# Two decode layers on one core: wo's last page in two transfers, and the gate's half without u done first

## The chip, the core and the metric

The kernel runs on one core of one Trainium2 chip. The metric is the device time of one execution in microseconds (us). Lower is better.

## What is computed

One token goes through two layers that share all weights. Each layer is an attention block over a key and value cache, and then a gated feed-forward block; both have a layernorm ahead and a residual around them:

```python
x = x + A(layernorm(x), k_cache, v_cache, wq, wo)
x = x + B(layernorm(x), w1, w3, w2)
x = x + A(layernorm(x), k_cache, v_cache, wq, wo)
x = x + B(layernorm(x), w1, w3, w2)

# A: 32 heads of 192, the last 4096 of 32768 cached positions, D = 640
q = x @ wq;  p = softmax(q . k * 192**-0.5);  out = concat(p . v) @ wo
# B: F = 1536
gate = x @ w1;  up = x @ w3;  out = (silu(gate) * up) @ w2
```

All data are bfloat16. Keys and values of the window are 1.5 MB a head each.

## The kernel before

**Memory.** `arena` holds 16 slots of one page, 128 x 6144 bf16 (1.5 MB). One list, `loads`, names all transfers of both layers in the order in which they are used: wq, the pages of keys and values, six pages of wo, then w1 (`fa`), w3 (`fb`), a mixed page `fc` (rest of w1, rest of w3, four chunks of w2) and `fd` (five more chunks of w2). The function `refill` takes the next entry whenever a slot is free and issues it on SP's queue; `done(key)` gives a slot back and calls it. The last three chunks of w2 (`keep`) and the last three chunks of wo's rows (`wo5`) are loaded in layer 0 and stay for layer 1. In layer 1, fourteen heads' keys are still on the chip. Each transfer on SP's queue waits, besides its slot, for the landing of the eighth transfer before it.

**Attention.** TensorE makes the scores of four heads in one accumulator, the softmax turns them, and the values are multiplied six heads later. `combine` leaves 48 columns in `otd`, one for each chunk of 128 rows of wo. `wo_proj` multiplies chunk after chunk into two accumulators, `y_ps`, four column groups at a time. Page w of six holds nine chunks, and the last page three. `y_to_residual` adds the result into `xsq`, and `layernorm` makes `xs` out of it.

**Feed-forward.** In `ffn`, `g_ps` collects x @ w1 and `u_ps` x @ w3: first four chunks of g (page `fa`), four of u (`fb`), then the fifth of g and of u (`fc`). Both are copied into `w20` as `gu`, g by ScalarE and u by VectorE, and are turned by three small matmuls each with `sel4` as the moving operand, into `gt_ps`, 24 columns of the one PSUM bank that `m_ps` lies in. Then VectorE and ScalarE make silu(g) * u out of it, in `htd`, twelve columns, one for each chunk of w2. In layer 0 the chunks of w2 are multiplied into `y2_ps`. In layer 1 `last_rows` does it: ten f32 matmuls bring the residual (`xw`, filled by GpSimd) into `f_ps`, 48 matmuls add the chunks of w2 in four column groups (a four of matmuls for each chunk), one cast follows, and the output leaves on SP's queue.

**What sets the order.** `pin` keeps every instruction in the order of the program on its engine, and `mm` does so for matmuls; all matmuls have the line of that helper, L80. So an engine runs what the code lists, in that order, and waits where its next instruction must. The framework adds the waits between engines, by what each instruction reads and writes.

The lines of the profile that matter here: L247 and L248 are the casts of y_ps, L242 writes xs, L444 and L445 are the copies of g and u, L451 is the exponential, L454 and L456 the copy into `ut` and the product `gut`, L458 and L459 the sum and the reciprocal, L460 writes `htd`, L489 is the last cast, L491 the output, and L210 issues pages.

Of the kernel before, what the change touches and what calls it, by code (L numbers as in the profile page):

```python
# [15 lines left out]
P = 128  # L16
# [31 lines left out]
def kernel(  # L48
# [79 lines left out]
    ptm = cst.tile([P, 16 * PW], BF16, name="ptm")  # L128
    otd = cst.tile([P, 48], BF16, name="otd")
    htd = cst.tile([P, 12], BF16, name="htd")  # L130
    zero = cst.tile([P, 32], BF16, name="zero")
    nc.gpsimd.memset(zero[:], 0.0)
    w20 = cst.tile([P, 768], BF16, name="w20")
    qt_sb = cst.tile([P, H, 6], BF16, name="qt_sb")
# [28 lines left out]
    for layer in range(2):  # L163
        for c in range(NCH):
            loads.append((("q", layer, c), [(0, PGW, wq_v[c])]))
        for i in range(H + LEAD):
            for kind, g, cache in (("v", i - LEAD, A_v_cache), ("k", i, A_k_cache)):
                if not 0 <= g < H:
                    continue
                h = head(layer, g)  # L170
                if kind == "k" and layer == 1 and h in RETAIN:
                    if h == STASH:
                        loads.append((("k", 1, h), []))
                    continue
                loads.append(((kind, layer, h),
                              [(0, PGW, cache[0, h, S0:SK, :].rearrange("(p t) d -> p (t d)", p=P))]))
        for w in range(6):
            parts = []
            for at, ci in enumerate(wo_order(layer)[9 * w:9 * w + 9]):
                blk, e = ORDER[layer][ci // 12], ci % 12  # L180
                if parts and parts[-1][2] == blk and parts[-1][3] + parts[-1][1] == e:
                    parts[-1][1] += 1
                else:
                    parts.append([at, 1, blk, e])
            parts = [(640 * at, 640 * n, wo_v[blk][:, 640 * e:640 * (e + n)]) for at, n, blk, e in parts]
            if w < 5:
                loads.append((("o", layer, w), parts))
            elif layer == 0:
                assert len(parts) == 1 and parts[0][1] == 1920
                loads.append((None, [(wo5[:], parts[0][2])]))  # L190
        loads.append((("fa", layer), [(0, PGW, w1_v[:, 0:PGW])]))
        loads.append((("fb", layer), [(0, PGW, w3_v[:, 0:PGW])]))
        loads.append((("fc", layer), [(0, 1536, w1_v[:, PGW:]), (1536, 1536, w3_v[:, PGW:]),
                                      (3072, 2560, w2_v[:, 0:2560])]))
        fd = [(0, 3200)] if layer == 0 else [(0, 1280), (1280, 1280), (2560, 640)]
        loads.append((("fd", layer), [(o, n, w2_v[:, 2560 + o:2560 + o + n]) for o, n in fd]))
        if layer == 0:
            loads.append((None, [(keep[:], w2_v[:, 5760:7680])]))
# [197 lines left out]

    def wo_proj(layer):
        y_ps = y_open("y_ps")
        for w in range(6):
            pg = page(("o", layer, w)) if w < 5 else wo5  # L400
            for cc, ci in enumerate(wo_order(layer)[9 * w:9 * w + 9]):
                n = 9 * w + cc
                j = n % 4
                for nh in range(2):
                    mm(y_ps[nh][32 * j:32 * j + 1, 0:320], lhsT=otd[:, ci:ci + 1],
                       rhs=pg[:, 640 * cc + 320 * nh:640 * cc + 320 * nh + 320],
                       start=False, stop=(n >= 44), tile_position=(0, 32 * j))
            if w < 5:
                done(("o", layer, w))
        y_to_residual(y_ps)  # L410
# [6 lines left out]
    def ffn(layer):  # L417
        if layer == 1:
            assert not loads
            spare = free[0] * PGW  # L420
            ident = arena[:, spare:spare + 64].bitcast(F32)
            nc.gpsimd.memset(ident, 0.0)
            for j in range(4):
                nc.gpsimd.affine_select(out=ident, in_=ident, compare_op=ALU.not_equal, fill=1.0, base=-32 * j,
                                        pattern=[[-1, 32]], channel_multiplier=1)
            xw = arena[:, spare + 64:spare + 64 + 1280].bitcast(F32)
            nc.gpsimd.memset(xw, 0.0)
            for j in range(4):
                nc.gpsimd.tensor_copy(out=xw[32 * j:32 * j + 32, 32 * j:640:128], in_=xsq[32 * j:32 * j + 32, 0:NCH])
            ident = (ident, xw)  # L430
        g_ps = ps_a.tile([P, 512], F32, tag="a", name="g_ps")
        u_ps = ps_a.tile([P, 512], F32, tag="a", name="u_ps")
        for ps, kind, c0, c1, off in ((g_ps, "fa", 0, 4, 0), (u_ps, "fb", 0, 4, 0),
                                      (g_ps, "fc", 4, 5, 0), (u_ps, "fc", 4, 5, 1536)):
            pg = page((kind, layer))
            for c in range(c0, c1):
                for j in range(4):
                    mm(ps[32 * j:32 * j + 32, 0:384], lhsT=xs[:, c, 3:35],
                       rhs=_ap(pg, 0, P, off + 1536 * (c - c0) + 3 * j, [[12, 128], [1, 3]]),
                       start=(c == 0), stop=(c == NCH - 1), tile_position=(0, 32 * j))  # L440
            if kind != "fc":
                done((kind, layer))
        gu = w20.rearrange("p (g n) -> p g n", g=2)
        pin(nc.scalar.copy(out=gu[:, 0, :], in_=g_ps[:, 0:384]))  # L444
        pin(nc.vector.tensor_copy(out=gu[:, 1, :], in_=u_ps[:, 0:384]))  # L445
        gt_ps = m_ps[:, 0:24].rearrange("p (g k j) -> p g k j", g=2, k=3)
        for gi in range(2):
            for k in range(3):
                mm(gt_ps[:, gi, k, :], lhsT=gu[:, gi, k:384:3], rhs=sel4[:], start=True, stop=True)
        ex = sml.tile([P, 12], F32, tag="ex", name="ex")  # L450
        pin(nc.scalar.activation(out=ex[:], in_=gt_ps[:, 0, :, :].rearrange("p k j -> p (k j)"), func=ACTF.Exp,  # L451
                                 scale=-1.0))
        ut = sml.tile([P, 12], F32, tag="ut", name="ut")
        pin(nc.vector.tensor_copy(out=ut[:], in_=gt_ps[:, 1, :, :].rearrange("p k j -> p (k j)")))  # L454
        gut = sml.tile([P, 12], F32, tag="gut", name="gut")
        pin(nc.vector.tensor_tensor(out=gut[:], in0=gt_ps[:, 0, :, :].rearrange("p k j -> p (k j)"), in1=ut[:],  # L456
                                    op=ALU.mult))
        pin(nc.vector.tensor_scalar_add(out=ex[:], in0=ex[:], scalar1=1.0))  # L458
        pin(nc.vector.reciprocal(out=ex[:], in_=ex[:]))  # L459
        pin(nc.vector.tensor_tensor(out=_ap(htd[:], 0, P, 0, [[1, 3], [3, 4]]),  # L460
                                    in0=gut[:].rearrange("p (k j) -> p k j", k=3),
                                    in1=ex[:].rearrange("p (k j) -> p k j", k=3), op=ALU.mult))
        if layer == 1:
            return last_rows(ident)
        y_ps = y_open("y2_ps")
        for fcx in range(12):
            j = fcx % 4
            pg, off = w2_chunk(layer, fcx)
            for nh in range(2):
                mm(y_ps[nh][32 * j:32 * j + 1, 0:320], lhsT=htd[:, fcx:fcx + 1], rhs=pg[:, off + 320 * nh:off + 320 * nh + 320],  # L470
                   start=False, stop=(fcx >= 8), tile_position=(0, 32 * j))
            if fcx == 3:
                done(("fc", layer))
        done(("fd", layer))
        y_to_residual(y_ps)

    def last_rows(ident):
        f_ps = ps_a.tile([P, 512], F32, tag="a", name="f_ps")
        eye, xw = ident
        for c in range(NCH):  # L480
            mm(f_ps[:, c:160:NCH], lhsT=xw[:, 128 * c:128 * c + 128], rhs=eye, start=(c == 0), stop=False)
        for fcx in (0, 1, 2, 3, 9, 10, 11, 4, 5, 6, 7, 8):
            pg, off = w2_chunk(1, fcx)
            for j in range(4):
                mm(f_ps[32 * j:32 * j + 1, 0:160], lhsT=htd[:, fcx:fcx + 1],
                   rhs=pg[:, off + 160 * j:off + 160 * j + 160],
                   start=False, stop=(fcx == 8), tile_position=(0, 32 * j))
        row = w20[:, 0:160]
        pin(nc.vector.tensor_copy(out=row, in_=f_ps[:, 0:160]))  # L489
        ps = row.ap[0][0]  # L490
        nc.sync.dma_start(out=out[0, 0, :].rearrange("(j i) -> j i", j=4),  # L491
                          in_=bass.AP(row.tensor, row.offset, [[32 * ps, 4], [1, 160]]))
# [69 lines left out]
```

## Time and profile before

| what | value |
|---|---|
| median of 3 runs | 528.83 us (528.5 to 529.74) |
| the profiled execution's own time | 528.32 us |
| its span | 526.6 us |
| moved by DMA | 221.97 MB, mean 421 GB/s |
| busy share of the span: PE, PEld, DVE, ACT, POOL | 52%, 21%, 49%, 12%, 3% |
| mean granted TensorE clock | 0.716 of full speed |

The span is the time from the first to the last instruction in the trace; the device time is 1.7 us longer. PE stands for TensorE's matmuls, PEld for its weight loads, DVE for VectorE, ACT for ScalarE, POOL for GpSimd and SP for the engine whose queue issues the transfers. A row of the timeline gives the start in us, the duration, engine, line, operation, output and inputs, shape and count; in brackets stand the idle time of the engine before it, and who ended it. A row of the windows gives a stretch, its length, busy time (and number of instructions) of PE, PEld, DVE, ACT and POOL, the granted clock, the share of DMA engines busy, and GB/s. In the rows of DMA queues the numbers are packets, MB and the share of 16 engines' span; in those of DMA issues, KB and the us from issue to landing.

### The profile page before, as it was taken

To read this page: it belongs to the slowest core of one execution; us is meant where nothing else is said; L and a number is where in the kernel's file an instruction comes from. 1 tells how busy PE (TensorE), PEld (TensorE's weight loads), DVE (VectorE), ACT (ScalarE), POOL (GpSimd) and SP (SyncE) were. 2 spreads that over 40 slices of the span, in tenths; PEclk is the share of its full clock that TensorE was granted. 3 is DMA by queue.
4 is the path that set the end of the run, shared out by engine and by line. 5 is a ranking of instruction groups with operands and counts; after the bars stand their busy time and mean duration, and the time that the engine had idled before them with its cause. 6 is when DMAs were issued, how large, how long until landed. Compare 5 with 4: busy or idle time off the path is not lost.

```text
span 526.6 us, 5978 instructions
## 1 busy us (share of the span) xinstructions
PE 275.0 (52%) x2403; PEld 112.6 (21%) x2403; DVE 256.4 (49%) x393; ACT 62.5 (12%) x192; POOL 16.2 (3%) x74
## 2 busy tenths in 40 slices
PE   2344644472655644455545555687254756345455
PEld 1111211131222221122112112233022322112113
DVE  1199676556657475654002139531475645753001
ACT  1002020110102020112001002022111120202000
POOL 4000000000000000000000000000000000001000
PEclk9997968666756776586556558988677886686557
DMA  8999999999999999999999999999999999999995
GB/s 349 429 430 433 426 428 427 433 432 427 427 428 432 432 426 429 428 432 423 419 431 422 427 428 427 420 431 427 428 428 431 429 428 429 429 431 428 424 432 242
DMA packets 22355, 221.97 MB, mean 421 GB/s; under 512 B 2616, under 2 KB 2744, under 8 KB 5176
## 3 DMA queue, kind: packets, MB, share of 16 engines
q1 hardware_dynamic: 22184, 221.59, 99.3%
q8 instruction: 19, 0.31, 0.2%
q14 instruction: 8, 0.07, 0.0%
q10 hardware_dynamic: 144, 0.00, 0.0%
HBM read 221.58 MB, written 0.00 MB: 421 GB/s over the span
## 4 chain that ended last, share of the span: by engine, by line
DMA 85%; PE 7%; DVE 5%; issue 1%; ACT 1%; SPq 1%; DVEq 0%; ACTq 0%
DMA arena<-in_A_k_cache_dram 51%; DMA arena<-in_A_v_cache_dram 16%; DMA arena<-in_A_wo_dram 9%; DMA arena<-in_B_w_dram 6%; DMA arena<-in_A_wq_dram 3%; DVE arena L300 3%; PE s_ps L80 3%; PE o_ps L80 2%; PE y_ps L80 1%; SPq L210 1%; PE q_ps L80 1%; PE u_ps L80 0%; PE pss L80 0%; ACT w L337 0%; DVE t L322 0%
## 5 line engine op out<-in xcount | busy, mean ns | idle before, releaser
L80 PE MATMUL s_ps<-arena,wst 128*32 128x512 bf16 x768 | 153.7, 512 | 171.3 <-DVE arena L300 84.5
L300 DVE STREAM_TRANSPOSE arena<-arena 128x1536 uint32<-128x1536 uint32 x100 | 171.2, 1754 | 75.0 <-DMA arena<-in_A_k_cache_dram 74.6
L80 PE MATMUL o_ps<-arena,ptm 128*8 128x384 bf16 (+1 forms) x1024 | 113.5, 421 | 12.9 <-DMA arena<-in_A_v_cache_dram 12.9
L80 PEld LDWEIGHTS <-wst 128*32 128x32 bf16 x768 | 53.1, 115 | 256.2 <-issue 227.1
L80 PEld LDWEIGHTS <-ptm 128*8 128x8 bf16 (+1 forms) x1024 | 40.0, 99 | 49.9 <-issue 40.3
L332 ACT ACTIVATE tb<-m 32x16 f32<-32x16 f32 x16 | 3.4, 214 | 280.4 <-DVE m L329 280.4
L350 ACT COPY ptm<-w 32x64 bf16<-32x64 bf16 x80 | 23.6, 295 | 42.5 <-PE o_ps L80 39.3
L80 PE MATMUL y_ps<-arena,otd 128*1 128x320 bf16 x180 | 16.9, 459 | 15.1 <-DMA arena<-in_A_wo_dram 15.1
L80 PE MATMUL q_ps<-arena,xs 128*32 128x512 bf16 x120 | 14.5, 624 | 17.3 <-DMA arena<-in_A_wq_dram 14.7
L383 DVE SCALAR_TENSOR_TENSOR w<-pss,rl,mask 64x192 bf16<-64x192 f32 x16 | 6.7, 417 | 32.2 <-PE pss L80 32.2
L282 POOL COPY wst<-qt_sb 32x24 bf16<-32x24 bf16 x30 | 8.4, 281 | 432.7 <-PE s_ps L80 313.8
L340 DVE STREAM_TRANSPOSE w<-w 64x512 bf16<-64x512 bf16 x16 | 11.3, 705 | 14.4 <-ACT w L337 14.4
L248 DVE CAST w<-y_ps 128x320 bf16<-128x320 f32 x3 | 1.5, 490 | 34.4 <-PE y_ps L80 34.4
L322 DVE TENSOR_REDUCE t<-s_ps 64x1 f32<-64x512 f32 x16 | 10.6, 663 | 12.2 <-PE s_ps L80 12.1
L274 DVE CAST qt_sb<-pss 32x192 bf16<-32x192 f32 x2 | 0.7, 346 | 31.2 <-PE pss L80 31.2
L350 DVE COPY ptm<-w 32x64 bf16<-32x64 bf16 x48 | 9.9, 207 | 10.8 <-PE o_ps L80 9.6
L80 PEld LDWEIGHTS <-xs 128*32 128x32 bf16 x200 | 7.2, 119 | 35.7 <-issue 26.1
L355 DVE RECIPROCAL rl<-pss 64x1 f32<-64x1 f32 x16 | 2.6, 166 | 22.2 <-PE pss L80 22.2
L80 PEld LDWEIGHTS <-otd 128*1 128x1 bf16 x192 | 6.4, 103 | 25.8 <-issue 21.7
L337 ACT ACTIVATE w<-s_ps,nbt 64x512 bf16<-64x512 f32 x16 | 10.9, 682 | 5.6 <-DVE nbt L334 5.6
L376 ACT CAST w<-o_ps 128x384 bf16<-128x384 f32 x16 | 7.7, 479 | 33.0 <-PE o_ps L80 23.7
L80 PE MATMUL pss<-w,sel 128*64 128x192 bf16 x32 | 6.3, 286 | 9.5 <-ACT w L376 6.4
(82 smaller groups left out, 111.8 us busy)
## 6 DMA issues: line engine op xcount, KB each, us to landing
arena<-in_A_v_cache_dram SPq DMA_DIRECT2D x64, 1536.0 KB, 29.2
arena<-in_A_k_cache_dram SPq DMA_DIRECT2D x50, 1536.0 KB, 29.2
arena<-in_A_wq_dram SPq DMA_DIRECT2D x10, 1536.0 KB, 9.3
arena<-in_A_wo_dram SPq DMA_DIRECT2D x6, 1440.0 KB, 15.3
arena<-in_B_w_dram SPq DMA_DIRECT2D x4, 1536.0 KB, 11.1
arena<-in_A_wo_dram SPq DMA_DIRECT2D x4, 960.0 KB, 16.8
arena<-in_A_wo_dram SPq DMA_DIRECT2D x4, 480.0 KB, 21.8
arena<-in_B_w_dram SPq DMA_DIRECT2D x4, 384.0 KB, 14.6
```

Of the source, the lines that this page charges most:

```text
L80: return pin(nc.tensor.matmul(*a, **k))
L210: pin(nc.sync.dma_start(out=arena[:, s * PGW + off:s * PGW + off + n], in_=src))
L282: pin((engs[a].copy if engs[a] is nc.scalar else engs[a].tensor_copy)(out=dst, in_=src))
L300: pin(nc.vector.transpose(x[:, w * sp:w * (sp + 1)].bitcast(U32), x[:, w * sp:w * (sp + 1)].bitcast(U32)))
L322: pin(nc.vector.reduce_max(out=t0[:, 0:1], in_=s_ps[0:64, :], axis=AX.X))
L332: pin(nc.scalar.mul(out=tb[32:64, :].rearrange("p (a z) -> p a z", a=4)[:, :, 0:HB], in_=mb, mul=-SCALE))
L337: pin(nc.scalar.activation(out=e[:], in_=s_ps[0:64, :], func=ACTF.Exp, bias=nbt[:, 0:1], scale=SCALE, accum_out=l[:]))
L340: pin(nc.vector.transpose(et[:], e[:]))
L350: pin((eng.copy if eng is nc.scalar else eng.tensor_copy)(out=dst, in_=src))
L355: pin(nc.vector.reciprocal(out=rl[half], in_=rl_ps[half]))
L376: pin(nc.scalar.copy(out=o_sb[:, 0:384], in_=o_ps[:, 0:384]))
L383: pin(nc.vector.scalar_tensor_tensor(out=om, in0=ot_ps[half], scalar=rl[half], in1=mask[half].unsqueeze(2).broadcast_to([64, 16, 12]), op0 ...
```

## The change

In layer 1 wo's page 4 (nine chunks) is loaded in two transfers, six chunks and three, into the same slot. The last page, `wo5`, which has long been on the chip, is multiplied before page 4 and not after it. In both layers the order of the gate is changed: g is copied and turned, the exponential, the sum, the reciprocal and the product g / (1 + exp(-g)) follow (into `ut`), and then u is turned and multiplied in one step from PSUM. The copy of u on VectorE still stands ahead of the gate's steps on that engine. The separate copy of u's turned half and the product `gut` are gone. In layer 1 the three kept chunks of w2 are multiplied first and not after the first four. `zero` is twice as wide.

```diff
-    zero = cst.tile([P, 32], BF16, name="zero")
+    zero = cst.tile([P, 64], BF16, name="zero")
...
+            if layer == 1 and w == 4:
+                (at, n, blk, e), = parts
+                parts = [[at, n - 3, blk, e], [at + n - 3, 3, blk, e + n - 3]]
...
-        for w in range(6):
+        for w in (0, 1, 2, 3, 4, 5) if layer == 0 else (0, 1, 2, 3, 5, 4):
             pg = page(("o", layer, w)) if w < 5 else wo5
             for cc, ci in enumerate(wo_order(layer)[9 * w:9 * w + 9]):
-                n = 9 * w + cc
+                n = 9 * w + cc if w < 4 or layer == 0 else cc + (36 if w == 5 else 39)
...
+        gu = w20.rearrange("p (g n) -> p g n", g=2)
+        gt_ps = m_ps[:, 0:24].rearrange("p (g n) -> p g n", g=2)
+        ex = sml.tile([P, 12], F32, tag="ex", name="ex")
+        ut = sml.tile([P, 12], F32, tag="ut", name="ut")
+
+        def turn(gi):
+            for k in range(3):
+                mm(gt_ps[:, gi, 4 * k:4 * k + 4], lhsT=gu[:, gi, k:384:3], rhs=sel4[:], start=True, stop=True)
+
+        def gate():
+            pin(nc.scalar.copy(out=gu[:, 0, :], in_=g_ps[:, 0:384]))
+            turn(0)
+            pin(nc.scalar.activation(out=ex[:], in_=gt_ps[:, 0, :], func=ACTF.Exp, scale=-1.0))
+            pin(nc.vector.tensor_scalar_add(out=ex[:], in0=ex[:], scalar1=1.0))
+            pin(nc.vector.reciprocal(out=ex[:], in_=ex[:]))
+            pin(nc.vector.tensor_tensor(out=ut[:], in0=gt_ps[:, 0, :], in1=ex[:], op=ALU.mult))
...
-        gu = w20.rearrange("p (g n) -> p g n", g=2)
-        pin(nc.scalar.copy(out=gu[:, 0, :], in_=g_ps[:, 0:384]))
         pin(nc.vector.tensor_copy(out=gu[:, 1, :], in_=u_ps[:, 0:384]))
-        gt_ps = m_ps[:, 0:24].rearrange("p (g k j) -> p g k j", g=2, k=3)
-        for gi in range(2):
-            for k in range(3):
-                mm(gt_ps[:, gi, k, :], lhsT=gu[:, gi, k:384:3], rhs=sel4[:], start=True, stop=True)
...
+        gate()
+        turn(1)
         pin(nc.vector.tensor_tensor(out=_ap(htd[:], 0, P, 0, [[1, 3], [3, 4]]),
-                                    in0=gut[:].rearrange("p (k j) -> p k j", k=3),
-                                    in1=ex[:].rearrange("p (k j) -> p k j", k=3), op=ALU.mult))
+                                    in0=gt_ps[:, 1, :].rearrange("p (k j) -> p k j", k=3),
+                                    in1=ut[:].rearrange("p (k j) -> p k j", k=3), op=ALU.mult))
...
-        for fcx in (0, 1, 2, 3, 9, 10, 11, 4, 5, 6, 7, 8):
+        for fcx in (9, 10, 11, 0, 1, 2, 3, 4, 5, 6, 7, 8):
```

## The prediction

> **What bounds the kernel now.** I read the page first, for who is busy all along.
>
> ```profile
> DMA  8999999999999999999999999999999999999995
> ...
> q1 hardware_dynamic: 22184, 221.59, 99.3%
> q8 instruction: 19, 0.31, 0.2%
> ```
>
> The 16 DMA engines are full from the second slice to the last half slice. So only two things can move the time: what the engines carry, and what is left after the last byte. Next come the windows of the tail, with granted clock (PEclk) and DMA share:
>
> ```profile
> 515.00:517.00 2.00, 1.35 (x16) 0.47 (x16) 0.29 (x1) 0.23 (x2) 0.00 (x0) 0.50 0.99 408
> ...
> 518.00:519.00 1.00, 1.00 (x18) 0.66 (x13) 0.00 (x0) 0.00 (x0) 0.00 (x0) 0.94 1.01 411
> ...
> 521.00:522.00 1.00, 1.00 (x10) 1.00 (x10) 0.66 (x5) 0.18 (x1) 0.00 (x0) 1.00 0.48 183
> 522.00:523.40 1.40, 1.26 (x50) 0.88 (x49) 0.18 (x1) 0.00 (x0) 0.00 (x0) 1.00 0.12 42
> ```
>
> DMA runs out between 520 and 523, and PE is full meanwhile. Which of them ends last is told by the DMA view of the last load's issue (160 KB, issued at 510.40; the last number is the us from issue to landing), and by the timeline:
>
> ```profile
> arena<-in_B_w_dram SPq DMA_DIRECT2D x1, 160.0 KB, 12.7
> ```
>
> ```profile
> 510.38 1.49 PE L80 MATMUL y_ps<-arena,otd 128*1 128x320 bf16 x17 [1.66 <-DMA arena<-in_A_wo_dram]
> ...
> 515.64 1.56 PE L80 MATMUL g_ps<-arena,xs 128*32 128x384 bf16 x16 [1.31 <-DVE xs L242]
> ...
> 517.72 1.23 PE L80 MATMUL u_ps<-arena,xs 128*32 128x384 bf16 x14 [0.52 <-DMA arena<-in_B_w_dram]
> ...
> 519.71 0.48 ACT L444 CAST w<-g_ps 128x384 bf16<-128x384 f32 x1 [4.45 <-PE g_ps L80]
> 520.14 0.56 DVE L445 CAST w<-u_ps 128x384 bf16<-128x384 f32 x1 [4.55 <-PE u_ps L80]
> ...
> 520.24 0.24 PE L80 MATMUL pss<-sel,w 128*128 128x4 bf16 x3 [0.16 <-ACT w L444]
> ...
> 520.75 0.24 PE L80 MATMUL pss<-sel,w 128*128 128x4 bf16 x3 [0.27 <-DVE w L445]
> ...
> 520.86 1.27 PE L80 MATMUL f_ps<-arena 128*128 128x32 f32 x10
> 521.03 0.18 ACT L451 ACTIVATE ex<-pss 128x12 f32<-128x12 f32 x1 [0.84 <-PE pss L80]
> ...
> 521.99 0.19 DVE L460 TENSOR_TENSOR htd<-gut,ex 128x12 bf16<-128x12 f32 x1
> 522.23 0.98 PEld L80 LDWEIGHTS <-htd 128*1 128x1 bf16 x48 [0.21 <-DVE htd L460]
> ...
> 522.72 0.65 PE L80 MATMUL f_ps<-arena,htd 128*1 128x160 bf16 x20
> 523.41 0.32 DVE L489 CAST w<-f_ps 128x160 bf16<-128x160 f32 x1 [1.23 <-PE f_ps L80]
> ```
>
> The 48 last matmuls go in twelve fours. 28 of them, seven fours, lie between 522.23 and 522.72: 0.07 us a four. The twelfth could start at 522.23 + 11 x 0.07 = 523.00. Its rows of w2 land at 510.40 + 12.7 = 523.1, and the group ends at 523.37, one matmul (0.23 by the tile's view) after 523.13. So the last transfer sets the end, with PE's chain only 0.13 us behind it. That slack decides this change.
>
> **The split of wo's page.** It adds one transfer, and no bytes. By the DMA view's landings the two-part page before it, 480 and 960 KB like the new pair, took 3.49 us (499.96 to 503.45); the whole pages after it took 3.42 (to 506.87 and 510.29). Price: 0.07 us on every later landing; bounds 0 and 0.1. One more issue on SP costs 0.33 there, and as each issue waits for the landing of the eighth transfer before it, w1's page is issued at 496.6 instead of 493.24. Its data are not due until 510.3, so this is hidden by over 10 us of queued transfers; the last load is still issued on the landing at 510.3.
>
> **Kept chunks first.** Behind the last wo landing stand 6 matmuls instead of 24, so y_ps, the layernorm and g_ps come about 1.1 us earlier (g_ps near 514.5). u_ps then still waits for its own transfer at 517.72, and the gap ahead of it grows from 0.5 to 1.7 us. Worth 0; were the cover gone, it would be 1.1. POOL's copies of the residual (done by 514.5) come earlier too, and nobody waits for them.
>
> **The gate.** Two DVE steps of 0.17 go (the copy into ut and one multiply). With the old durations and gaps: the g copy ends at 520.19, g's turn runs 520.24 to 520.48, the exponential 520.52 to 520.70. DVE is in the u cast until 520.70, then add, reciprocal and multiply (0.17, 0.23, 0.17, 0.03 apart) end at 521.37.
>
> Now what the diff does not say. In the built program the first matmul of u's turn waits, beyond its weights, for the DVE count that this multiply sets. It writes columns 12 to 23 while the multiply reads 0 to 11, of one bank: ordered, though no data need it. So u's turn starts at about 521.42, not 520.75. PE works in order, and behind it are queued the ten f32 matmuls that bring the residual into f_ps, which until now ran under the exponential. The last step on DVE follows u's turn, and htd is ready at 521.90 instead of 522.18. But PE is not free: the old rows have the first f32 matmul 0.11 us after u's turn began and the last 1.00 later (1.27 less one of 0.276), and one more step of 0.11. The w2 matmuls start at 521.42 + 1.22 = 522.64, not 522.23. Moving the kept chunks to the front covers only the landing of the others, which are in by then. The twelfth four starts at 522.64 + 0.77 = 523.41 and ends at 523.65, against 523.37: +0.28, and the bound changes from transfer to PE.
>
> **Layer 0.** The same shift makes htd about 0.3 us earlier there (288.6 to 288.3; the f32 matmuls do not exist, only two y2 openers of 0.43 in all). The w2 matmuls of that layer then wait for transfers anyway (289.45, 0.31 idle on DMA). A slot comes free 0.3 us sooner, but DMA is full there. Worth 0, and 0.3 without that cover. `zero` grows just as `gut` goes, and the arena keeps its address: 0.
>
> **Sum.** 0.07 + 0.28 = +0.35 us on the profiled 528.32 gives 528.67. The runs' median lies 0.51 above the profiled run, so 529.18, or 529.2. About 0.2% (1.06 us) is what a measurement of this kernel can tell from no change, so this counts as the same.
>
> **Rivals.**
> *The clock rises late (slower).* In the tail it goes from 0.50 to 1.00 near 518.1 (0.94 in that window). In layer 0:
>
> ```profile
> 279.00:282.50 3.50, 1.59 (x17) 0.47 (x16) 0.69 (x3) 0.41 (x2) 0.00 (x0) 0.50 0.95 402
> 282.50:286.00 3.50, 1.92 (x20) 0.82 (x21) 0.00 (x0) 0.48 (x1) 0.00 (x0) 0.50 1.05 424
> ```
>
> Sixteen such matmuls in 3.5 us did not raise it, twenty did, at 286. Before 518.1 there were also about twenty. The change pulls g_ps earlier, so about two of them leave that stretch: eighteen, between the two. If the rise comes one stretch later (near 521.5), u_ps takes 1.57 instead of 1.23 us (layer 0's row) and the last g and u chunks 0.1 to 0.2 more: +0.5 ahead of the gate, 0.9 in all with the 0.35, and up to 1.4 if five of the f32 matmuls are at half clock too (5 x 0.11): 529.7 to 530.2. It counts as slower from the point where the delay ahead of u's turn passes 0.7. Against it: twenty is no known threshold, and the kernel before may meet late rises as well. The Trainium skill (TensorE: Matmul & The Clock Gate, The HAM clock gate) has a free-running window of 3413 ns that must be busy for the clock to rise; the two stretches above agree, and by it the outcome differs from run to run.
> *The last transfer still sets the end.* If PE passes the f32 matmuls faster or the wait costs nothing, only 0.07 is left: 528.9. Against it stand 0.28 us of PE work.
> *A split transfer pays its start alone (slower).* The lone output transfer takes 1.7 us (issue at 523.80, then SP waits 1.0 behind 0.65): +1.7 + 0.35, 530.9. The 3.49 us of the two-part page speaks against it. The Trainium skill (DMA: Bandwidth & Descriptors, Anatomy of one DMA) puts about 2.0 us of fixed cost on each DMA, of the GpSimd path; by that it would be 531.2. The landings do not show it.
> *Instruction packets.* 0.2% of 16 engines' 526.6 us over 19 packets is 0.9 us each, in the way of one engine. One more on the engine that ends last: 530.1. Two fewer: 527.4, the only way to clearly faster that I see, since no step of the change reaches the transfers.
>
> **Chances.** Forecast 0.52, late clock 0.24, transfer still last 0.10, lone start 0.03, packets 0.06 worse and 0.05 better. Within 0.2%: 0.48 of the forecast (0.04 goes over by scatter; three runs spread over 1.24 us), half the late clock, 0.10: 0.70. Slower: 0.04 + 0.12 + 0.03 + 0.06 = 0.25. Faster: 0.05. The range runs from the transfer-bound case less the scatter (528.3) to a late clock at its dearest and 0.3 of scatter (530.5).
>
> **What would show it.** Right: u's turn starts behind the multiply, after 521.3; the f32 matmuls follow it; no wait for DMA before the last four w2 matmuls; htd earlier yet the last matmul later. Wrong: an end still released by the last transfer, a DMA idle stretch after the split page, or a window with clock 0.50 past 518.5 (late clock). A time below 527.8 would refute the whole account.

## The result and the profile after

The changed kernel is slower: 530.21 us median (22 runs) against 528.73 us (22 runs), a ratio of 1.0029 with a 95% interval of 1.0022 to 1.0036, that is +1.5 us. The profiled execution took 529.69 us with a span of 527.9 us; the one before had 528.32 and 526.6.

The tail of layer 1 in the timeline of the kernel after:

```profile
514.57 1.58 PE L80 MATMUL g_ps<-arena,xs 128*32 128x384 bf16 x16 [1.32 <-DVE xs L245]
...
517.72 1.25 PE L80 MATMUL u_ps<-arena,xs 128*32 128x384 bf16 x14 [1.57 <-DMA arena<-in_B_w_dram]
...
520.50 0.18 ACT L448 ACTIVATE ex<-pss 128x12 f32<-128x12 f32 x1 [0.33 <-PE pss L80]
...
521.26 0.17 DVE L451 TENSOR_TENSOR ut<-pss,ex 128x12 f32<-128x12 f32 x1
521.48 0.22 PE L80 MATMUL pss<-sel,w 128*128 128x4 bf16 x3 [1.01 <-DVE ut L451]
...
521.59 1.27 PE L80 MATMUL f_ps<-arena 128*128 128x32 f32 x10
521.74 0.19 DVE L466 TENSOR_TENSOR htd<-pss,ut 128x12 bf16<-128x12 f32 x1 [0.31 <-PE pss L80]
...
522.79 0.38 PE L80 MATMUL f_ps<-keep,htd 128*1 128x160 bf16 x12
523.00 0.80 PE L80 MATMUL f_ps<-arena,htd 128*1 128x160 bf16 x36
523.85 0.32 DVE L495 CAST w<-f_ps 128x160 bf16<-128x160 f32 x1 [1.92 <-PE f_ps L80]
524.23 0.66 SPq L497 DMA_DIRECT2D out_dram<-w  x1
```

The order up to the last matmul is the one that was forecast. g_ps is 1.1 us earlier and the gap ahead of u_ps grows by as much. u's turn stands idle for 1.01 us until the multiply into `ut` is through. `htd` is ready at 521.93, 0.25 us earlier than before, but the f32 matmuls now run behind u's turn, and the w2 matmuls start at 522.79 and not 522.23. They wait for no transfer any more: the 36 run through in 0.80 us, and the last load, issued at 510.41, takes 12.7 us as before. The last matmul ends at 523.80, where before it was 523.37: +0.43 us.

But the span grew by 1.3 us. The rest lies behind that matmul. What SP waited for at the end, before and then after (waits of SP's queue: us in total, times, longest):

```profile
SPq L557 <- DMA out_dram<-w: 1.0, 1, 1.0
```

```profile
SPq L563 <- DMA out_dram<-w: 1.9, 1, 1.9
```

The output, 1.2 KB in both kernels, is 0.9 us longer on its way. The page's row of the queue q14, which like q8 carries instructions, has one packet more within the span, before and then after:

```profile
q14 instruction: 8, 0.07, 0.0%
```

```profile
q14 instruction: 9, 0.07, 0.0%
```

The DMA view of the stretch from 523.5 to 527 says what shares the engines with the output after; before, from 520 to the end, there was, besides q1's own packets, only one of q8.

```profile
q8 instruction: 1, 0.02, 2.3%
q14 instruction: 1, 0.01, 1.0%
q1 hardware_dynamic: 8, 0.00, 0.2%
```

In the trace the q14 packet (8 KB) starts at 525.35 and takes 0.56 us. Three of the output's four pieces start between 525.49 and 525.51, the fourth at 525.91, where that packet ends. Before, the packet of the same kind starts at 527.25, behind the end of the program. So 0.43 us on TensorE and 0.9 us on the output account for the 1.3 us of the span. How the last piece, 0.4 us late, comes to hold SP for 0.9 us longer no run tells.

### The profile page after: what moved, and what is told of

Its sections match the earlier page's. It is cut to its first block, busy times and chain, and to the rows that moved or that the text cites. A ratio compares the mean times of both kernels' runs of the same rounds, so it can differ in the third digit from the quotient of the medians.

```text
span 527.9 us, 5982 instructions
## 1 busy us (share of the span) xinstructions
PE 275.2 (52%) x2403; PEld 112.6 (21%) x2403; DVE 256.2 (49%) x391; ACT 62.5 (12%) x192; POOL 16.2 (3%) x74
## 4 chain that ended last, share of the span: by engine, by line
DMA 85%; PE 8%; DVE 5%; ACT 1%; issue 1%; SPq 1%; DVEq 0%; ACTq 0%
DMA arena<-in_A_k_cache_dram 51%; DMA arena<-in_A_v_cache_dram 16%; DMA arena<-in_A_wo_dram 9%; DMA arena<-in_B_w_dram 6%; DMA arena<-in_A_wq_dram 3%; PE s_ps L80 3%; DVE arena L303 3%; PE o_ps L80 2%; PE y_ps L80 1%; SPq L213 1%; PE q_ps L80 1%; PE u_ps L80 0%; PE pss L80 0%; PE f_ps L80 0%; ACT w L340 0%
## 5 line engine op out<-in xcount | busy, mean ns | idle before, releaser
L80 PE MATMUL o_ps<-arena,ptm 128*8 128x384 bf16 (+1 forms) x1024 | 114.7, 420 | 12.5 <-DMA arena<-in_A_v_cache_dram 12.4
```

Of the source, the lines that this page charges most:

```text
L80: return pin(nc.tensor.matmul(*a, **k))
```

## Experiments

**Theory A** has two causes: the order on TensorE (u's turn waits, the f32 matmuls behind it), and a block of instructions that VectorE asks for while the output is under way. The trace has 450 instructions on VectorE after and 448 before, those that only wait or drain included (the page, which leaves them out, has 391 and 393): in each layer the new gate has one operation less, but two instructions that only wait. **Theory B** is TensorE's queue alone. The **late clock** of the prediction is the third. "Against before" is the median of runs of the kernel before on the same chip; the bounds are the interval of the ratio times that median. Each version ran 11 or 12 times, gate_only 5 times, and the kernel after 22 times.

| kernel | median | before | against before by the ratio | VectorE's instructions |
|---|---|---|---|---|
| after | 530.21 | 528.73 | +1.5 us (1.2 to 1.9) | 450 |
| b_plus1 | 528.80 | 528.63 | +0.3 (-0.2 to 0.7) | 449 |
| b_plus2 | 529.64 | 528.95 | +0.6 (0.2 to 1.1) | 450 |
| b_plus8 | 529.23 | 528.95 | +0.1 (-0.4 to 0.5) | 456 |
| a_minus2 | 529.78 | 528.95 | +0.7 (0.3 to 1.2) | 448 |
| a_plus6 | 529.28 | 528.63 | +0.6 (0.1 to 1.1) | 456 |
| a_f32first | 529.73 | 528.95 | +0.6 (0.2 to 1.1) | 450 |
| wo_only | 528.69 | 528.75 | -0.2 (-0.6 to 0.3) | 448 |
| gate_only | 530.61 | 528.75 | +1.7 (1.1 to 2.3) | 450 |
| a_f32first_minus2 | 528.58 | 528.75 | -0.1 (-0.5 to 0.3) | 448 |
| g_f32first_minus2 | 528.68 | 528.75 | -0.1 (-0.5 to 0.4) | 448 |

### Instructions that do nothing, added to the kernel before

```diff
+    for _ in range(2):                       # b_plus2; 8 in b_plus8, 1 in b_plus1
+        nc.vector.memset(onesb[:], 1.0)
     nc.vector.tensor_copy(out=xsq[:, 0:NCH], in_=xb[:])
```

> The kernel before, with two more memsets of one column on VectorE at the start, while it waits for x. Theory A (code block): the two traces differ by 0.43 us at the last matmul and by about 1.0 us between the issue of the output and its landing, where the trace after has an instruction packet of 8 KB at 525.35 beside one piece of the output; the trace before has that packet at 527.25, past its end. VectorE has 450 instructions after and 448 before, so two more are enough: +0.9 to +1.0 us (529.7), the instruction packet ahead of the last output piece, PE's end unchanged. Theory B (TensorE's queue alone, with or without a late clock): 0.0 us.

> The kernel before, with eight more such memsets. Theory A: the block is asked for six instructions sooner, in the gate near 521.5, and is in before the output leaves: +0.0 us, at most +0.5 if it lies on the DMA engine that ends last; the time comes back although there are more instructions. If more VectorE instructions as such cost time: at least as much as two do. Theory B: 0.0 us.

> The kernel before with one more such memset. Theory A: the instruction that asks for the block is then the last but one of the program on VectorE, behind the landing of the output, and not the wait ahead of it: 0.0 us, and SP waits 1.0 us for the output. If each instruction adds its share: half of what two added, +0.3 us.

SP's wait for the output in b_plus2, and the packet beside it:

```profile
SPq L559 <- DMA out_dram<-w: 1.8, 1, 1.8
```

```profile
q14 instruction: 1, 0.01, 0.4%
```

The same wait in b_plus8 and in b_plus1:

```profile
SPq L559 <- DMA out_dram<-w: 1.0, 1, 1.0
```

```profile
SPq L559 <- DMA out_dram<-w: 1.0, 1, 1.0
```

Two memsets at the start of a kernel that is otherwise untouched lengthen the output's way at the end of it by 0.8 us; one does nothing, and eight do nothing. TensorE's last matmul keeps its place behind the last load (it ends 0.28 us after the landing, as in the kernel before) in all three. In b_plus8's trace the packet has moved to 517.04, under the loads, in b_plus1's it is at 527.15, behind the end. That is theory A's mechanism, and theory B is out as the only cause.

The traces also show when the packet comes. In nine of the ten with 448 to 450 instructions it starts 1.10 to 1.14 us after VectorE's 447th instruction has ended, so when the 448th comes up (1.39 us in the tenth, a_f32first_minus2). In a program of 448 the 448th is the last one, behind the landing of the output; of 449, the last but one; of 450, it is the wait for that landing, which comes up while the output is on its way (524.22 in the trace after). In the two programs of 456 the packet comes while VectorE still waits for u_ps (517.04 and 515.62).

The size by the medians is smaller than expected, +0.6 and not 0.9 to 1.0, with an interval that holds both.

### The same in the kernel after

```diff
-    nc.vector.memset(onesD[:], 1.0 / D)      # a_minus2
+    nc.gpsimd.memset(onesD[:], 1.0 / D)
-    nc.vector.memset(onesb[:], 1.0)
+    nc.gpsimd.memset(onesb[:], 1.0)
...
+    for _ in range(6):                       # a_plus6, with both memsets on VectorE
+        nc.vector.memset(onesb[:], 1.0)
```

> The kernel after, with two memsets at the start (onesD, onesb) on GpSimd and not on VectorE, so that VectorE has as many instructions as before. Theory A: the instruction packet falls behind the end again, and 0.9 to 1.0 us of the 1.5 go: +0.4 to +0.5 us against before (529.2), which is TensorE's part. Theory B: as after, +1.5 us.

> The kernel after with six more memsets of one column on VectorE at the start. Theory A: VectorE's block is asked for six instructions sooner, ahead of the output, and the output lands 0.9 us sooner than in the kernel after although the program is longer: +0.5 to +1.0 us against before, as with two instructions fewer, not +1.5. If the number of instructions as such costs time: +1.5 us or more.

Two fewer and six more do the same: SP waits 0.9 us again in both, here in a_plus6,

```profile
SPq L565 <- DMA out_dram<-w: 0.9, 1, 0.9
```

and by the medians 0.8 to 0.9 of the 1.5 us go. A longer program is faster. What stays, 0.6 to 0.7 us with intervals from 0.1 to 1.2, is a little more than the 0.43 of the profile; the run of the gate alone offers a reason.

### Each half alone

`wo_only` has the new wo and the old `ffn`; `gate_only` the new `ffn` (with the wider `zero`) and the old wo.

```diff
-            if layer == 1 and w == 4:                    # left out in gate_only
-                (at, n, blk, e), = parts
-                parts = [[at, n - 3, blk, e], [at + n - 3, 3, blk, e + n - 3]]
...
-        for w in (0, 1, 2, 3, 4, 5) if layer == 0 else (0, 1, 2, 3, 5, 4):
+        for w in range(6):
```

> The kernel before with the change of wo alone (page 4 in two transfers, kept chunks ahead of it); the gate is the old one. Theory A (two causes, TensorE's order at the end and VectorE's next block of code): VectorE has as many instructions as before and the gate's order is old, so neither cause is here: 0.0 to +0.1 us. Rival (the earlier g_ps starves the clock gate): a clock that rises late in some runs, +0.2 to +0.5 us.

> The kernel before with the new gate and the kept chunks of w2 first; wo as before. Theory A: both causes are here (VectorE has two more instructions, u's turn waits), so +1.4 to +1.5 us, all of the change, and in the trace an instruction packet beside the output. Rival (the earlier g_ps starves the clock gate): +0.9 to +1.2 us, since g_ps is as late as before.

All of the loss is in the gate (+1.7 us, where +1.4 to +1.5 was expected); the split of the page and the earlier g_ps are worth nothing that can be measured. This ends the late clock as it was forecast, since in gate_only g_ps is as late as before. But the clock does enter. Windows of gate_only (columns as in the prediction; the number behind the bracketed counts is PEclk), and its last matmuls in the timeline:

```profile
522.00:523.00 1.00, 1.00 (x10) 1.00 (x10) 0.19 (x1) 0.00 (x0) 0.00 (x0) 1.00 0.12 44
523.00:524.00 1.00, 1.00 (x34) 0.95 (x37) 0.00 (x0) 0.00 (x0) 0.00 (x0) 0.51 0.00 0
```

```profile
521.77 0.22 PE L80 MATMUL pss<-sel,w 128*128 128x4 bf16 x3 [1.01 <-DVE ut L448]
...
523.08 0.57 PE L80 MATMUL f_ps<-keep,htd 128*1 128x160 bf16 x12
523.43 1.41 PE L80 MATMUL f_ps<-arena,htd 128*1 128x160 bf16 x36
```

The clock was not late (it rose at 519.6), it fell at 523.0, one stretch of 3.4 us later, ahead of the w2 matmuls: they take 1.76 us and not 1.01. In that stretch TensorE stood idle 1.01 us for the multiply. The last matmul ends 1.57 us behind the last landing, where before it was 0.28 us. The trace of a_minus2 shows the same (clock up from 519.8 to 523.2, last matmul 1.31 us behind the last landing). wo_only and g_f32first_minus2, whose clock rose at 519.98 and 519.94 and whose TensorE doesn't wait there, kept it until 526.8. In after and a_plus6, which have the wait, it rose at 518.0 and 519.0 and held too. So against the last landing the wait costs 0.4 us (after, a_plus6), or 1.0 to 1.3 where the clock falls (a_minus2, gate_only). In these four traces it fell in the two where it had risen last; whether the place of the rise decides is not shown beyond them. How often it falls in runs without a profile stays open.

### The f32 matmuls ahead of u's turn

```diff
         gate()
+        f_ps = last_open(ident) if layer == 1 else None   # opens f_ps, ten f32 matmuls
         turn(1)
```

> The kernel after, with the ten f32 matmuls of layer 1 between g's turn and u's turn, so that they run while u's turn waits. Theory A: the last four matmuls wait for the last transfer again (523.1), the last matmul ends at 523.4 and not 523.8: 0.4 us less than after, +1.0 us against before (529.7), with the late output. Theory B: all of it goes, 0.0 to +0.1 us. Late clock: the time stays near +1.5, since the clock would still rise late in most runs.

> The kernel after with the ten f32 matmuls ahead of u's turn and the two memsets on GpSimd. Theory A: both causes are gone, and what is left is the gate that is 0.3 us shorter, ahead of a last transfer that sets the end: -0.1 to +0.1 us against before (528.9). Rival (something else in the change costs time too): over +0.3 us.

> The same without the change of wo. Theory A: -0.2 to 0.0 us against before; the split is worth 0.07 us at most, so not to be told from the run with it. If earlier g_ps helps or hurts: the two differ by 0.3 us or more.

`a_f32first` has this edit alone. `a_f32first_minus2` has the two memsets on GpSimd as well, and `g_f32first_minus2` also leaves out the change of wo. TensorE's queue in the timeline of a_f32first_minus2:

```profile
520.26 0.24 PE L80 MATMUL pss<-sel,w 128*128 128x4 bf16 x3
520.37 1.53 PE L80 MATMUL f_ps<-arena 128*128 128x32 f32 x10
521.73 0.22 PE L80 MATMUL pss<-sel,w 128*128 128x4 bf16 x3
522.23 0.38 PE L80 MATMUL f_ps<-keep,htd 128*1 128x160 bf16 x12 [0.28 <-DVE htd L467]
522.44 0.91 PE L80 MATMUL f_ps<-arena,htd 128*1 128x160 bf16 x36
```

The f32 matmuls fill the wait, the w2 matmuls start as early as in the kernel before, and the last 36 wait for the last transfer again (0.91 instead of 0.80). In a_f32first the output still meets the packet (SP waits 1.8 us), and +0.6 us are left, somewhat less than expected. In all three traces the last matmul ends 0.28 us behind the last landing, as in the kernel before. With both causes gone the kernel is as fast as the one before, with the split or without it, and not faster. The gate is not even shorter there: u's turn now stands behind the f32 matmuls (521.73, and 521.77 without the split), so the w2 matmuls start at 522.23 and 522.26, no earlier than before, and the last transfer sets the end. No version that was run beats the kernel before beyond its interval.

## Why the prediction was right and where it was wrong

The range (528.3 to 530.5) held 530.21, but by luck: its upper end was worked out from a late clock, and the larger part of the loss in the profile came from something else. The forecast itself, 529.2 and no measurable change, did not hold: +1.5 us where it had +0.35. What failed in the sum is that it has nothing for a block of code beside the output; in the profile that is 0.9 us.

- **The split, 0.07 us, and the cover of the kept chunks.** Right. The last load was issued at 510.4 and took 12.7 us in both kernels; wo_only is at -0.2 us with an interval around 0. u_ps starts at 517.72 in both traces.
- **Layer 0.** No sign of a gain or loss; g_f32first_minus2, which has the new gate there too, is at -0.1 us.
- **TensorE's order.** Right in every step: u's turn behind the multiply, the f32 matmuls behind u's turn, the bound going from transfer to TensorE. The size was 0.28 and is 0.43 in the profile. Mis-sized were the last step of the f32 group, taken as 0.11 and measured as 0.20 to the first w2 matmul, and the multiply, which starts 0.06 later than summed; the trace has one of the instructions that only wait ahead of it, at 521.19. Where the clock falls it is 1.0 to 1.3 us, which no part of the prediction had. The gain of 0.25 us in htd is real in the trace after, but worth nothing, since the w2 matmuls stand behind the f32 matmuls.
- **What was missing.** The step "two DVE steps of 0.17 go" was wrong in its count (one operation goes in each layer, since one of the two products only moves) and counted operations, not instructions. The built program has two instructions more on VectorE, and by that its next block of code is fetched while the output is under way: 0.9 us. The rival of the instruction packets had the price (0.9) and even the sum (530.1), but gave it a chance of 0.06, as an accident on the engine that ends last among the loads. The price agrees by luck: it is the mean of q8's 16 KB packets, thought of as a delay among the loads, and the packet that did the harm is one of q14, 8 KB, which takes 0.56 us and which the prediction does not speak of. It is no accident either: the packet lies beside the output in all four traces with 450 instructions on VectorE (after, b_plus2, gate_only, a_f32first), where the output's last piece starts within 0.02 us of the packet's end, and in none of the eight with 448, 449 or 456.
- **The late clock.** It had the next largest chance, and its reason fell: the rise was on time in the profile after, and the gate alone loses as much without an earlier g_ps. The clock costs time by another way, a fall behind TensorE's wait.
- **A split transfer that pays its start alone.** Refuted by wo_only.

The Trainium skill (Runtime: NRT & Kernel Launch, Instruction fetch mechanics) says that an engine's code is fetched in blocks while it runs and that crossing a block is mostly hidden. The one that meets the output is not hidden here: it costs 0.8 to 0.9 us by SP's waits. What the other eight of q14 cost among the loads no run tells. The Trainium skill (DMA: Bandwidth & Descriptors, Queues, rings and completion order) has the completion of a transfer land only after every earlier write from that DMA engine. That could be where the rest goes, since the last piece starts 0.4 us late and SP waits 0.9 us longer; no run here shows it.

## What to carry to other kernels

Count instructions of the built program, those that only wait too, and not operations of the source: on an engine that works in order, a reordering that looks shorter can put a wait ahead of work that used to fill the gap, so look at what stands behind the wait. When a small change moves the end by about a microsecond that no engine's work explains, look at the last, lonely transfer and at what shares the DMA engines with it; adding a few instructions that do nothing at the start tells whether a fetch of code is the cause.

## What was not expected of the hardware

A program got faster by about 0.9 us when six instructions were added to it (a_plus6 at +0.6 us, after at +1.5), and another slower by 0.6 us by two (b_plus2): the 8 KB block of one engine's code, 0.45 to 0.56 us on a DMA engine in the four traces where it meets the output, holds up 1.2 KB by 0.8 to 0.9 us. And the granted clock fell to half 3.4 us after its rise when TensorE stood idle for 1.01 us in that stretch of light matmuls (gate_only, a_minus2: busy for 2.2 to 2.3 us of it), while it held at the same place without that wait (wo_only, g_f32first_minus2: busy for 2.9 us). The wait is not the whole rule: after and a_plus6 have the same wait and 2.3 us in the stretch behind the rise, and held, and b_plus1, without the wait, fell at 523.7 behind 2.6 us, when its last matmul was over. What the clock goes by stays open. Its last rise ahead of the w2 matmuls came anywhere from 518.0 to 522.0 in the traces, whatever the kernel. That agrees with the free-running window of the Trainium skill (TensorE: Matmul & The Clock Gate, The HAM clock gate); its rule that the clock falls after an idle window does not fit here, if idle means without work, since TensorE was busy for 2.2 us of the 3.4 in gate_only (519.61 to 523.02).
